# Decode attention with a gated MLP: order and pieces of the last loads, and where wo's rows are placed and multiplied

## The chip, the cores and the metric

One core of a Trainium2 chip runs the kernel. The metric is the device time of one execution in microseconds. A core has TensorE (PE; its weight loads are listed apart as PEld), VectorE (DVE), ScalarE (ACT), GpSimd (POOL) and SyncE (SP), each with its own instruction stream, and sixteen DMA engines that move data from HBM. Transfers that SP issues go through one queue (q1 in the profile), those that GpSimd issues through another (q0); both are served by the same sixteen engines.

## The reference

One token is decoded. Attention has 32 heads of 128 with 4096 cached keys and values each; beside it runs an MLP with a squared ReLU, and a sigmoid gate mixes the two. All tensors are bfloat16.

```python
g = sigmoid((x * gate_w).sum(-1, keepdims=True))          # x: 1 x 512
q = (x @ wq).reshape(1, 1, 32, 128).transpose(0, 2, 1, 3) # wq: 512 x 4096
p = softmax(einsum("bhqd,bhkd->bhqk", q, k) * 128**-0.5)  # k: 32 x 4096 x 128
o = einsum("bhqk,bhkd->bhqd", p, v)                       # v: 32 x 4096 x 128
a = o.transpose(0, 2, 1, 3).reshape(1, 1, 4096) @ wo      # wo: 4096 x 512
h = relu(x @ w1 + b1) ** 2                                # w1: 512 x 1376
b = h @ w2 + b2                                           # w2: 1376 x 512
out = g * a + (1 - g) * b
```

Keys and values are 32 MB each; with the weights, 78 MB are read for one row of 512 outputs.

## The kernel before

**Tiles and loads.** Four heads make one tile: `k_v` and `v_v` give each of NT = 8 tiles as 128 partitions of 32 KB (32 partitions a head, 128 key or value rows in each partition). A ring of SLOTS = 5 buffers of that size holds them. LOADS (L125) is the order: k0, k1, then k two tiles ahead of v, and ahead of v7 a slot "m" for what is used at the end (w1, w2, the last rows of wo). SP issues the loads in this order (L318 to L343), each after `free` (L300) has seen the slot's last reader finish. The v tiles in PARTS are issued in pieces, each with a semaphore of its own: v6 in four, v7 in four unequal ones. Behind them come the last 512 rows of wo (`wob_sb`, two transfers, L339) and the last 128 rows of w2 (`w2b`, L341). The wait in `pv` for the pieces is at L542.

**Scores, softmax, values.** Of the 128 blocks of a k tile VectorE multiplies and sums 80 (`ttr`, L711); the others are transposed on TensorE (L509), evacuated by ScalarE (L415) and multiplied on TensorE (L522). The maximum goes through `max_rows`, `gmax` and `max_cols` (L529, L725, L728, L534), ScalarE takes the exponentials (L434), and `pv` (L553) multiplies the values block by block. `den`, `recip` and `norm` divide by the sum. A loop over NU = 32 units (four to a tile) interleaves these by hand on every engine.

**wo.** Its first 3584 rows (28 heads) are loaded in mid-run into W, in the place of wq: a chunk is 32 rows of wo, 32 KB, in one partition, and 112 of the 128 partitions get one. A run `(kind, e, k, r, m)` in RUNS or FIRST is a transfer of chunks to partitions p, p + st, ...: `place` (L90) gives the start, the step and the count. e, from 0 to 15, numbers the first of k neighbours in a circle of sixteen; INNER lies in partitions 32 to 95, OUTER below 32 (e < 8) and from 96 up, SEAM joins partitions 28 + r and 96 + r (e = 7 and 8), WRAP joins r and 124 + r (e = 15 and 0). RUNS are issued by GpSimd (L378), FIRST by SP ahead of the fifth load (L327). `turns` (L99) keeps a count modulo 16 of where GpSimd's next transfer starts: a transfer of k chunks moves it by k, and where a run is to start elsewhere a tiny transfer (L375) of d rows into `dm` moves it by d. FIRST's run `(OUTER, 4, 1, 3, 1)` is one chunk alone, in partition 19.

Which chunk lies in which partition is undone by the matrix `selA` (one affine_select a run, L363): at the end `turn_a` and `spread_a` (L566, L572) turn the first 28 heads' outputs into `o2A`, 32 columns in the partitions' order.

**The end.** In program order on TensorE (L649 to L667): `turn_a`, `max_rows(7)`, `spread_a`, `out_a`, which multiplies TP = 22 of the 32 columns with W (88 matmuls, L580), `max_cols(7)`, `mlp_h` (w1, 44 matmuls, L594), `den`, `mlp_out(0..9)` (w2's first 1280 rows, 40 matmuls, L605), then the four `pv` of v7 with `add_v` before the second of them, `out_b` (the last four heads, 16 matmuls, L614) and `mlp_out(10)` (4 matmuls). All of them add up in one PSUM tile, `acc`. VectorE in the meantime (`rows_v`, L763) multiplies the other TV = 10 columns with W, 512 wide, into `vsum`, with the MLP's activation in between (`mlp_bias`, `mlp`); `add_v` (L583) sums `vsum` over the partitions on TensorE. Then VectorE adds the bias (L814), TensorE transposes (L667), and SP writes the result (L343).

Of the kernel before, what the change touches and what calls it, by code (L numbers as in the profile page):

```python
# [5 lines left out]
def bass_gated_mix__gqa_block_cached__dense_activation_squared_relu__decode_kernel(  # L6
# [50 lines left out]
    for i in (28, 29, 30):  # L57
# [3 lines left out]

    PARTS = {NT - 3: [0, 64, B], NT - 2: [0, 32, 64, 96, B], NT - 1: [0, 40, 80, 116, B]}

# [10 lines left out]
    NZ = NH - NA  # L74
    TS = [0, 3, NZ]

    TV = 10
    TP = 32 - TV
    TM = 6
    INNER, OUTER, SEAM, WRAP = range(4)  # L80
    RUNS = [(INNER, 4, 12, 0, 2), (INNER, 4, 12, 1, 2),
            (OUTER, 4, 3, 0, 1), (SEAM, 7, 2, 0, 1), (OUTER, 9, 7, 0, 1), (OUTER, 4, 3, 1, 1),
            (SEAM, 7, 2, 1, 1), (OUTER, 9, 7, 1, 1), (OUTER, 4, 3, 2, 1),
            (SEAM, 7, 2, 2, 1), (OUTER, 9, 7, 2, 1),
            (SEAM, 7, 2, 3, 1), (WRAP, 15, 2, 3, 1), (OUTER, 1, 2, 3, 1)]
    FIRST = [(INNER, 0, 3, 0, 1), (INNER, 0, 3, 1, 1), (INNER, 0, 3, 2, 1), (INNER, 0, 3, 3, 1),
             (OUTER, 0, 3, 0, 1), (OUTER, 0, 3, 1, 1), (OUTER, 0, 3, 2, 1),
             (OUTER, 4, 1, 3, 1)]

    def place(kind, e, k, r, m):  # L90
        if kind == INNER:
            return 32 + 4 * e + r, 4 // m, k * m
        if kind == OUTER:
            return (4 * e if e < 8 else 64 + 4 * e) + r, 4, k
        if kind == SEAM:
            return 28 + r, 68, k
        return r, 124, k

# [22 lines left out]
    w1_v = B_w1.rearrange("(p t) n -> p (t n)", t=4)  # L121
    w2_v = B_w2[0:FG * 128, :].rearrange("(p g) n -> p (g n)", g=FG)

# [11 lines left out]
    with ctx:  # L135
# [24 lines left out]
        oA, fin4 = [held("m")[0:p, W5 + n * 128:W5 + n * 128 + 128] for n, p in enumerate((NA, 4))]  # L160
        vsum = held("k", NT - 1)[:, 0:2 * DM].bitcast(fp32)

# [19 lines left out]
        selA = sb("selA", [NA, 4, 128], bf16)  # L182
        o2f = sb("o2f", [128, TV], fp32)
        dm = sb("dm", [16, len(RUNS), 2, 6], bf16)
# [53 lines left out]
        s_l = [sem(f"s_l{i}") for i in range(SLOTS)]  # L238
        s_w = [sem(f"s_w{n}") for n in range(3)]
        s_wo = [sem(f"s_wo{n}") for n in range(len(TS) - 1)]  # L240
        s_wp = [sem(f"s_wp{n}") for n in range(len(RUNS))]
# [40 lines left out]
        s_h = sem("s_h")  # L282
        s_vs = sem("s_vs")
        s_hv = sem("s_hv")
# [32 lines left out]
        @block.sync  # L317
        def _(eng):  # L318
            for n, (kind, j) in enumerate(LOADS):
                free(eng, n)  # L320
                if n == SLOTS - 1:
                    started(eng)
                    for p, st, k, q in STRIPS[len(RUNS):]:
                        a, b = W[p:p + st * (k - 1) + 1:st, :], woa_v[q:q + k, :]
                        if k == 1:
                            a, b = [v.rearrange("p (a n) -> p a n", a=2) for v in (a, b)]
                        eng.dma_start(a, b).then_inc(s_wr, 16)  # L327
                if kind == "v" and j in PARTS:
                    for w in range(len(PARTS[j]) - 1):
                        part = slice(PARTS[j][w] * 128, PARTS[j][w + 1] * 128)  # L330
                        eng.dma_start(held("v", j)[:, part], v_v[j][:, part]).then_inc(s_vl[j, w], 16)  # L331
                elif kind in "kv":
                    eng.dma_start(held(kind, j), (k_v if kind == "k" else v_v)[j])\
                       .then_inc(s_l[n % SLOTS], 16)
                elif kind == "m":
                    eng.dma_start(held("m")[:, 0:W2], w1_v).then_inc(s_w[0], 16)
                    eng.dma_start(held("m")[:, W2:W3], w2_v).then_inc(s_w[1], 16)  # L337
            for c in range(len(TS) - 1):
                eng.dma_start(wob_sb[:, TS[c]:TS[c + 1], :], wob_v[:, TS[c]:TS[c + 1], :])\  # L339
                   .then_inc(s_wo[c], 16)  # L340
            eng.dma_start(w2b, B_w2[F - 128:F, :]).then_inc(s_w[2], 16)  # L341
            eng.wait_ge(s_f4, 1)
            eng.dma_start(out[0, 0, :].rearrange("(j p) -> j p", p=128), fin4).then_inc(s_out, 16)  # L343
# [110 lines left out]
        def _(eng):  # L454
# [11 lines left out]
            for n in range(FG + 1):  # L466
                mm = eng.matmul(B1[:, n:n + 1], b1r[:, n:FG * 128:FG] if n < FG else b1r[:, F - 128:F],
                                ident[0:1, 0:1], start=True, stop=True)
            mm.then_inc(s_b1, 1)
# [67 lines left out]
            def pv(u):  # L537
                j, w = u // U, u % U
                lo, hi = w * B // U, (w + 1) * B // U
                if j == NT - 1:  # L540
                    lo, hi = PARTS[j][w:w + 2]
                if j in PARTS:  # L542
# [32 lines left out]

            def out_a():
                eng.wait_ge(s_ac, 2)
                for t in range(TP):
                    for j in range(4):
                        eng.matmul(acc[:, j:j + 1], wo_sb[:, t, j * 128:(j + 1) * 128], o2A[:, t:t + 1],  # L580
                                   start=(t == 0 and j == 0), stop=False, skip_group_check=True)

            def add_v():  # L583
                eng.wait_ge(s_vs, TV)
                for j in range(4):
                    eng.matmul(acc[:, j:j + 1], vsum[:, j * 128:(j + 1) * 128], onesf[:, 0:1],
                               start=False, stop=False, skip_group_check=True)

            def mlp_h():
                eng.wait_ge(s_w[0], 16)  # L590
                for n in range(FG + 1):
                    for t in range(4):
                        lhs = w1_sb[:, t, n:FG * 128:FG] if n < FG else w1_sb[:, t, F - 128:F]
                        mm = eng.matmul(H[:, n:n + 1], lhs, xcol[:, t:t + 1],  # L594
                                        start=(t == 0), stop=(t == 3))
                mm.then_inc(s_h, 1)

            def mlp_out(n):
                if n in (0, FG):
                    eng.wait_ge(s_w[1 if n < FG else 2], 16)  # L600
                if n == 0:
                    eng.wait_ge(s_hs, 1)
                w = w2a[:, n, :] if n < FG else w2b
                for j in range(4):
                    mm = eng.matmul(acc[:, j:j + 1], w[:, j * 128:(j + 1) * 128], hs[:, n:n + 1],  # L605
                                    start=False, stop=(n == FG), skip_group_check=True)
                if n == FG:
                    mm.then_inc(s_acc, 1)

            def out_b(c):  # L610
                eng.wait_ge(s_wo[c], 16)
                for h in range(TS[c], TS[c + 1]):
                    for j in range(4):
# [37 lines left out]
            spread_a()  # L651
            out_a()
            max_cols(NT - 1)
            mlp_h()
            den(NG - 1)
            for n in range(FG):
                mlp_out(n)
            for u in range((NT - 1) * U, NU):
                if u == NU - 3:
                    add_v()  # L660
                pv(u)
            eng.wait_ge(s_on, NG)
            for c in range(len(TS) - 1):
                out_b(c)
            mlp_out(FG)
            eng.wait_ge(s_fin, 1)
# [4 lines left out]
        def _(eng):  # L671
# [90 lines left out]

            def rows_v():  # L763
                eng.wait_ge(s_ac, 3)
                eng.wait_ge(s_sd, NU)
                eng.wait_ge(s_t, 2 * NU)
                eng.wait_ge(s_wk, 1)
                for t in range(TV):
                    if t == TM:
                        mlp_bias()  # L770
                        mlp()
                    if t == 0:
                        eng.tensor_scalar(vsum[:, :], wo_sb[:, TP, :], o2f[:, 0:1], None, ALU.mult)\
                           .then_inc(s_vs, 1)
                    else:
                        eng.wait_ge(s_vs, t)
                        eng.scalar_tensor_tensor(out=vsum[:, :], in0=wo_sb[:, TP + t, :],
                                                 scalar=o2f[:, t:t + 1], in1=vsum[:, :],
                                                 op0=ALU.mult, op1=ALU.add).then_inc(s_vs, 1)

            for c in range(EARLY - 1):
# [24 lines left out]
            eng.tensor_copy(o2A[:, :], O2A).then_inc(s_ac, 1)  # L806
            eng.tensor_copy(o2f[:, :], O2A[:, TP:32]).then_inc(s_ac, 1)
            gmax(NT - 1)
            rows_v()
            recip(NG - 1)  # L810
# [37 lines left out]
```

## Time and profile before

| what | value |
|---|---|
| three runs | 192.72, 192.87, 193.0 us, median 192.87 |
| the profiled execution | 192.9 us, of which the page's span is 191.5 |
| bytes moved | 78.74 MB, mean 411 GB/s |
| granted TensorE clock over the run | 0.581 |
| VectorE: `ttr` (L711) | 656 multiply-reduces of 280 ns and 656 accumulator reads of 76 ns; last one ends at 172.4 us |
| VectorE: `rows_v` (L773, L777) | 174.31 to 183.07 us, 0.49 us and nine of 0.75 us |
| SP: issue of v7's pieces, wob, w2b | 150.6 to 174.9 us |
| GpSimd: 14 runs of wo and 7 tiny transfers | issued 33.8 to 46.1 us, last one landed at 112.8 |
| one packet on a DMA engine, 32 KB | 1.213 us |
| 16 KB, 10 KB, 9 KB, 8 KB | 0.611, 0.387, 0.349, 0.310 us |
| 3 KB, 1 KB, a semaphore's 4 bytes | 0.121, 0.046, 0.009 us |

The span is what the hardware profiler saw of the kernel's instructions; the execution's own time has 1.4 us around it. A packet is one contiguous piece of one partition. The slices of the page are a fortieth of the span, 4.8 us, each; a digit is the busy share in tenths. Busy times in a table by stages are followed by the number of instructions.

### The profile page before, as it was taken

How to read it: one execution, taken by the hardware profiler on the slowest of the kernel's cores; microseconds unless marked ns; L12 is line 12 of the kernel's file. 1: busy time of each engine (PE TensorE's matmuls, PEld its weight loads, DVE VectorE, ACT ScalarE, POOL GpSimd, SP SyncE). 2: the span in 40 equal slices, each digit the busy share in tenths (PEclk: the TensorE clock that was granted, in tenths of full speed). 3: DMA queues.
4: the chain of work that ended last, by engine and by line, in shares of the span. 5: the costliest groups of instructions: out<-in, count | busy, mean ns of one | idle time of the engine just before them, and what ended most of it. 6: DMA issues, size and time to landing. Idle time of an engine off the chain costs nothing.

```text
span 191.5 us, 6005 instructions
## 1 busy us (share of the span) xinstructions
PE 111.0 (58%) x2058; PEld 97.6 (51%) x2058; DVE 159.0 (83%) x1387; ACT 82.7 (43%) x204; POOL 22.7 (12%) x56
## 2 busy tenths in 40 slices
PE   0129667545614653397569145933887478648975
PEld 0123335535503542297459145933877268537964
DVE  0320399999999999899999998998999799998821
ACT  2105765843833663087349222941663393000400
POOL 7760000996000000000000000000000000000000
PEclk9999985855555555555555555555555555555555
DMA  6999999999999999999999999999999999999992
GB/s 226 432 438 438 438 440 428 438 411 450 411 443 411 421 412 421 438 429 431 414 447 421 428 426 428 431 417 424 428 419 424 411 428 409 421 415 428 417 382 70
DMA packets 5488, 78.74 MB, mean 411 GB/s; under 512 B 1285, under 2 KB 1927, under 8 KB 2056
## 3 DMA queue, kind: packets, MB, share of 16 engines
q1 hardware_dynamic: 4484, 75.40, 92.9%
q0 software_dynamic: 960, 2.95, 3.9%
q8 instruction: 16, 0.26, 0.6%
q14 instruction: 14, 0.11, 0.1%
q10 hardware_dynamic: 14, 0.01, 0.0%
HBM read 78.35 MB, written 0.00 MB: 409 GB/s over the span
## 4 chain that ended last, share of the span: by engine, by line
DVE 48%; DMA 40%; SPq 7%; PE 3%; issue 1%; DVEq 0%
DVE ring L711 45%; DMA ring<-in_A_k_cache_dram 26%; DMA ring<-in_A_wo_dram 14%; SPq L331 6%; DVE S L711 2%; PE pO L553 1%; PE KP L509 1%; DVE gm L725 1%; DVE gx L728 0%; PE pM L562 0%; PE pM L534 0%; PE pQ L614 0%; SPq L337 0%; SPq L294 0%; DVE mp L718 0%
## 5 line engine op out<-in xcount | busy, mean ns | idle before, releaser
L711 DVE CUSTOM_DVE_ANT_0 ring<-ring,qb 128x128 bf16<-128x128 bf16 x656 | 140.6, 280 | 2.9 <-DMA ring<-in_A_k_cache_dram 2.9
L415 ACT ACTIVATE kT<-KP 128x768 bf16<-128x768 bf16 (+1 forms) x64 | 46.4, 783 | 48.1 <-PE KP L509 47.8
L509 PE MATMUL KP<-ident,ring 128*128 128x128 bf16 x368 | 43.4, 302 | 23.2 <-DMA ring<-in_A_k_cache_dram 19.9
L711 DVE DVE_READ_ACCUMULATOR2_ANT S<- 128x1 f32 x656 | 49.7, 76 | 0.1
L509 PEld LDWEIGHTS KP<-ident,ring 128*128 128x128 bf16 x368 | 36.0, 140 | 25.9 <-DMA ring<-in_A_k_cache_dram 20.4
L553 PE MATMUL pO<-E,ring 128*128 128x4 bf16 x640 | 19.5, 167 | 2.9 <-DMA ring<-in_A_v_cache_dram 1.9
L553 PEld LDWEIGHTS pO<-E,ring 128*128 128x128 bf16 x640 | 18.7, 105 | 3.4 <-DMA ring<-in_A_v_cache_dram 2.1
L434 ACT ACTIVATE E<-S,nM 32x128 bf16<-32x128 f32 x32 | 18.5, 580 | 0.9
L553 PE MATMUL pX<-E,ring 128*128 128x4 bf16 x384 | 12.0, 167 | 4.6 <-DMA ring<-in_A_v_cache_dram 4.6
L553 PEld LDWEIGHTS pX<-E,ring 128*128 128x128 bf16 x384 | 11.4, 105 | 5.1 <-DMA ring<-in_A_v_cache_dram 4.9
L426 ACT ACTIVATE nM<-pM 128x1 f32<-128x1 f32 x8 | 1.4, 172 | 23.0 <-PE pM L534 23.0
L529 PE MATMUL pM<-identf,mp 128*1 128x128 f32 x8 | 3.1, 384 | 13.0 <-DVE mp L718 13.0
L534 PE MATMUL pM<-onesf,gx 1*128 1x1 f32 x16 | 4.6, 357 | 8.9 <-DVE gx L728 8.9
L534 PEld LDWEIGHTS pM<-onesf,gx 1*128 1x128 f32 x16 | 4.0, 306 | 9.6 <-DVE gx L728 9.6
L522 PE MATMUL pQ<-qcol,kT 128*128 128x4 bf16 x176 | 7.8, 170 | 1.0 <-ACT kT L415 0.9
L522 PEld LDWEIGHTS pQ<-qcol,kT 128*128 128x128 bf16 x176 | 7.6, 111 | 1.4 <-ACT kT L415 1.4
L434 ACT ACTIVATION_READ_ACCUMULATOR E<-S,nM 32x1 f32 x32 | 8.1, 253 | 0.0
L522 PE MATMUL pS<-qcol,kT 128*128 128x4 bf16 x192 | 8.1, 169 | 0.0
L386 POOL MEMSET tick<- 1x1 f32 x1 | 0.1, 88 | 66.8 <-DMA W<-in_A_wo_dram 66.8
L378 POOL DMA_DIRECT2D W<-in_A_wo_dram x14 | 8.0, 572 | 0.0
L529 PEld LDWEIGHTS pM<-identf,mp 128*1 128x1 f32 x8 | 0.7, 92 | 14.2 <-DVE mp L718 14.0
L522 PEld LDWEIGHTS pS<-qcol,kT 128*128 128x128 bf16 x192 | 7.8, 108 | 0.2
(83 smaller groups left out, 97.3 us busy)
## 6 DMA issues: line engine op xcount, KB each, us to landing
ring<-in_A_k_cache_dram SPq DMA_DIRECT2D x8, 4096.0 KB, 30.4
ring<-in_A_v_cache_dram SPq DMA_DIRECT2D x5, 4096.0 KB, 29.7
W<-in_A_wq_dram SPq DMA_DIRECT2D x1, 4096.0 KB, 12.4
ring<-in_A_v_cache_dram SPq DMA_DIRECT2D x2, 2048.0 KB, 27.7
ring<-in_A_v_cache_dram SPq DMA_DIRECT2D x4, 1024.0 KB, 27.5
ring<-in_A_v_cache_dram SPq DMA_DIRECT2D x2, 1280.0 KB, 31.4
W<-in_A_wo_dram POOLq DMA_DIRECT2D x2, 768.0 KB, 17.8
ring<-in_B_w_dram SPq DMA_DIRECT2D x1, 1376.0 KB, 24.8
```

Of the source, the lines that this page charges most:

```text
L331: eng.dma_start(held("v", j)[:, part], v_v[j][:, part]).then_inc(s_vl[j, w], 16)
L378: eng.dma_start(W[p:p + st * (k - 1) + 1:st, :], woa_v[q:q + k, :], max_dma_last_dim=16384).then_inc(s_wp[n], 16)
L415: eng.activation(kT[:, n % NC, 0:HB[u // U] * 128], KP[n % 3][:, 0:HB[u // U] * 128], ACT.Copy).then_inc(s_ev, 1)
L426: eng.activation(nM[:, j:j + 1], MB[:, j:j + 1], ACT.Copy).then_inc(s_nm, 1)
L434: eng.activation(E[rows, j % NE, :, r], S[rows, j % NS, :], ACT.Exp, bias=nM[rows, j:j + 1], scale=SCALE, accum_out=RS[rows, R * j + r:R * ...
L509: mm = eng.transpose(KP[n % 3][:, y * 128:(y + 1) * 128], held("k", j)[:, b * 128:(b + 1) * 128], ident[:, :])
L522: mm = eng.matmul(S2[j % 2][:, c:c + R], kT[:, n % NC, y * 128:(y + 1) * 128], qcol[:, R * j:R * j + R], start=True, stop=True)
L529: eng.transpose(MT[0:1, :], mp[:, j:j + 1], identf[:, :]).then_inc(s_mt, 1)
L534: eng.matmul(MB[:, j:j + 1], gx[0:1, j % 2, :], onesf[0:1, 0:1], start=True, stop=True).then_inc(s_mb, 1)
L553: mm = eng.matmul(O(R * j, R * j + R), held("v", j)[:, b * 128:(b + 1) * 128], E[:, j % NE, b, :], start=(b == 0), stop=(b == B - 1), skip ...
L711: ins = eng.tensor_tensor_reduce(kb, kb, qb[:, j, :], 1.0, 0.0, ALU.mult, ALU.add, S[:, j % NS, b:b + 1])
L725: eng.tensor_reduce(g, MT[0:1, :].rearrange("a (r p) -> a r p", r=R), AX.X, ALU.max)\
```

## The change

Five things change, and nothing of what is computed.

- **Order and pieces of the last loads.** w1 stays ahead of v7. w2's first 1280 rows come behind v7 and behind wob, and in two transfers, of 8 and of 2 groups of 128 rows, each with its semaphore; then the last 128 rows as before. wob is one transfer. v6 and v7 come in two pieces, 96 and 32 blocks.
- **TensorE's order at the end.** The first 8 columns of `out_a`, `max_cols(7)`, the other 24 columns, `mlp_h`, `den`, the four `pv` of v7 in equal quarters, `out_b`, and then all of `mlp_out`.
- **wo's rows.** VectorE's part of them (`rows_v`, `vsum`, `o2f`) and `add_v` go; `out_a` multiplies all 32 columns (128 matmuls).
- **Chunks.** RUNS has ten runs instead of fourteen (88 chunks instead of 90), FIRST has eight of three chunks each instead of seven and a single one (24 instead of 22). WRAP and the single chunk go.
- **w1's and w2's groups.** A column of H belongs to w2's new groups: `group(n)` gives the columns of w1 and b1 (stride 8 for n < 8, stride 2 for the next two, the last 128 as before).

```diff
-    PARTS = {NT - 3: [0, 64, B], NT - 2: [0, 32, 64, 96, B], NT - 1: [0, 40, 80, 116, B]}
+    PARTS = {NT - 3: [0, 64, B], NT - 2: [0, 96, B], NT - 1: [0, 96, B]}
+
+    FE = 8
...
     RUNS = [(INNER, 4, 12, 0, 2), (INNER, 4, 12, 1, 2),
-            (OUTER, 4, 3, 0, 1), (SEAM, 7, 2, 0, 1), (OUTER, 9, 7, 0, 1), (OUTER, 4, 3, 1, 1),
-            (SEAM, 7, 2, 1, 1), (OUTER, 9, 7, 1, 1), (OUTER, 4, 3, 2, 1),
-            (SEAM, 7, 2, 2, 1), (OUTER, 9, 7, 2, 1),
-            (SEAM, 7, 2, 3, 1), (WRAP, 15, 2, 3, 1), (OUTER, 1, 2, 3, 1)]
+            (OUTER, 4, 4, 0, 1), (OUTER, 8, 8, 0, 1), (OUTER, 4, 4, 1, 1), (OUTER, 8, 8, 1, 1),
+            (OUTER, 4, 4, 2, 1), (OUTER, 8, 8, 2, 1),
+            (OUTER, 3, 2, 3, 1), (SEAM, 7, 2, 3, 1)]
     FIRST = [(INNER, 0, 3, 0, 1), (INNER, 0, 3, 1, 1), (INNER, 0, 3, 2, 1), (INNER, 0, 3, 3, 1),
-             (OUTER, 0, 3, 0, 1), (OUTER, 0, 3, 1, 1), (OUTER, 0, 3, 2, 1),
-             (OUTER, 4, 1, 3, 1)]
+             (OUTER, 0, 3, 0, 1), (OUTER, 0, 3, 1, 1), (OUTER, 0, 3, 2, 1), (OUTER, 0, 3, 3, 1)]
+
+    def group(n):
+        a, b, s = ((0, FE * 128, FE) if n < FE else (FE * 128, FG * 128, FG - FE) if n < FG else
+                   (F - 128, F, 1))
+        return slice(a + (n if n < FE else n - FE if n < FG else 0), b, s)
...
-    w2_v = B_w2[0:FG * 128, :].rearrange("(p g) n -> p (g n)", g=FG)
+    w2_v = [B_w2[a * 128:b * 128, :].rearrange("(p g) n -> p (g n)", g=b - a) for a, b in ((0, FE), (FE, FG))]
...
                 elif kind == "m":
                     eng.dma_start(held("m")[:, 0:W2], w1_v).then_inc(s_w[0], 16)
-                    eng.dma_start(held("m")[:, W2:W3], w2_v).then_inc(s_w[1], 16)
-            for c in range(len(TS) - 1):
-                eng.dma_start(wob_sb[:, TS[c]:TS[c + 1], :], wob_v[:, TS[c]:TS[c + 1], :])\
-                   .then_inc(s_wo[c], 16)
-            eng.dma_start(w2b, B_w2[F - 128:F, :]).then_inc(s_w[2], 16)
+            eng.dma_start(wob_sb, wob_v).then_inc(s_wo, 16)
+            for c, (a, b) in enumerate(((0, FE), (FE, FG))):
+                eng.dma_start(held("m")[:, W2 + a * DM:W2 + b * DM], w2_v[c]).then_inc(s_w[1 + c], 16)
+            eng.dma_start(w2b, B_w2[F - 128:F, :]).then_inc(s_w[3], 16)
...
             spread_a()
-            out_a()
+            out_a(0, TM)
             max_cols(NT - 1)
+            out_a(TM, 32)
             mlp_h()
             den(NG - 1)
-            for n in range(FG):
+            for u in range((NT - 1) * U, NU):
+                pv(u)
+            out_b()
+            for n in range(FG + 1):
                 mlp_out(n)
-            for u in range((NT - 1) * U, NU):
-                if u == NU - 3:
-                    add_v()
-                pv(u)
-            eng.wait_ge(s_on, NG)
-            for c in range(len(TS) - 1):
-                out_b(c)
-            mlp_out(FG)
...
             eng.tensor_copy(o2A[:, :], O2A).then_inc(s_ac, 1)
-            eng.tensor_copy(o2f[:, :], O2A[:, TP:32]).then_inc(s_ac, 1)
             gmax(NT - 1)
-            rows_v()
+            mlp_bias()
+            mlp()
             recip(NG - 1)
             norm(NG - 1)
```

TM is 8 after the change. `mlp_out(n)` waits for its piece of w2 at n = 0, 8 and 10, and `out_b` for the norm and for wob.

More of the change, by code (lines that the diff above doesn't have):

```diff
@@ L74, in bass_gated_mix__gqa_block_cached__dense_activation_squared_relu__decode_kernel @@
     NZ = NH - NA
[L75 to L80, printed above, removed]
+    TM = 8
+    INNER, OUTER, SEAM = range(3)
     RUNS = [(INNER, 4, 12, 0, 2), (INNER, 4, 12, 1, 2),
-            (OUTER, 4, 3, 0, 1), (SEAM, 7, 2, 0, 1), (OUTER, 9, 7, 0, 1), (OUTER, 4, 3, 1, 1),
-            (SEAM, 7, 2, 1, 1), (OUTER, 9, 7, 1, 1), (OUTER, 4, 3, 2, 1),
-            (SEAM, 7, 2, 2, 1), (OUTER, 9, 7, 2, 1),
-            (SEAM, 7, 2, 3, 1), (WRAP, 15, 2, 3, 1), (OUTER, 1, 2, 3, 1)]
+            (OUTER, 4, 4, 0, 1), (OUTER, 8, 8, 0, 1), (OUTER, 4, 4, 1, 1), (OUTER, 8, 8, 1, 1),
+            (OUTER, 4, 4, 2, 1), (OUTER, 8, 8, 2, 1),
+            (OUTER, 3, 2, 3, 1), (SEAM, 7, 2, 3, 1)]
     FIRST = [(INNER, 0, 3, 0, 1), (INNER, 0, 3, 1, 1), (INNER, 0, 3, 2, 1), (INNER, 0, 3, 3, 1),
-             (OUTER, 0, 3, 0, 1), (OUTER, 0, 3, 1, 1), (OUTER, 0, 3, 2, 1),
-             (OUTER, 4, 1, 3, 1)]
+             (OUTER, 0, 3, 0, 1), (OUTER, 0, 3, 1, 1), (OUTER, 0, 3, 2, 1), (OUTER, 0, 3, 3, 1)]
[3 more added lines that the diff above has]
+        return slice(a + (n if n < FE else n - FE if n < FG else 0), b, s)
     def place(kind, e, k, r, m):
@@ L94, in place @@
             return (4 * e if e < 8 else 64 + 4 * e) + r, 4, k
-        if kind == SEAM:
-            return 28 + r, 68, k
-        return r, 124, k
+        return 28 + r, 68, k
     def turns():
@@ L160, in bass_gated_mix__gqa_block_cached__dense_activation_squared_relu__decode_kernel @@
         oA, fin4 = [held("m")[0:p, W5 + n * 128:W5 + n * 128 + 128] for n, p in enumerate((NA, 4))]
-        vsum = held("k", NT - 1)[:, 0:2 * DM].bitcast(fp32)
         start = ring[:, SLOTS - 1, :]
@@ L182, in bass_gated_mix__gqa_block_cached__dense_activation_squared_relu__decode_kernel @@
         selA = sb("selA", [NA, 4, 128], bf16)
-        o2f = sb("o2f", [128, TV], fp32)
         dm = sb("dm", [16, len(RUNS), 2, 6], bf16)
@@ L238, in bass_gated_mix__gqa_block_cached__dense_activation_squared_relu__decode_kernel @@
         s_l = [sem(f"s_l{i}") for i in range(SLOTS)]
-        s_w = [sem(f"s_w{n}") for n in range(3)]
-        s_wo = [sem(f"s_wo{n}") for n in range(len(TS) - 1)]
+        s_w = [sem(f"s_w{n}") for n in range(4)]
+        s_wo = sem("s_wo")
         s_wp = [sem(f"s_wp{n}") for n in range(len(RUNS))]
@@ L282, in bass_gated_mix__gqa_block_cached__dense_activation_squared_relu__decode_kernel @@
         s_h = sem("s_h")
-        s_vs = sem("s_vs")
         s_hv = sem("s_hv")
@@ L323, in _ @@
                     for p, st, k, q in STRIPS[len(RUNS):]:
[L324 to L327, printed above, removed]
+                        eng.dma_start(W[p:p + st * (k - 1) + 1:st, :], woa_v[q:q + k, :]).then_inc(s_wr, 16)
                 if kind == "v" and j in PARTS:
@@ L466, in _ @@
             for n in range(FG + 1):
-                mm = eng.matmul(B1[:, n:n + 1], b1r[:, n:FG * 128:FG] if n < FG else b1r[:, F - 128:F],
-                                ident[0:1, 0:1], start=True, stop=True)
+                mm = eng.matmul(B1[:, n:n + 1], b1r[:, group(n)], ident[0:1, 0:1], start=True, stop=True)
             mm.then_inc(s_b1, 1)
@@ L539, in pv @@
                 lo, hi = w * B // U, (w + 1) * B // U
-                if j == NT - 1:
-                    lo, hi = PARTS[j][w:w + 2]
                 if j in PARTS:
@@ L574, in spread_a, with out_a @@
                 mm.then_inc(s_at, 1)
-            def out_a():
+            def out_a(a, b):
                 eng.wait_ge(s_ac, 2)
-                for t in range(TP):
+                for t in range(a, b):
                     for j in range(4):
@@ L581, in out_a @@
                                    start=(t == 0 and j == 0), stop=False, skip_group_check=True)
[L583 to L587, printed above, removed]
             def mlp_h():
@@ L592, in mlp_h @@
                     for t in range(4):
-                        lhs = w1_sb[:, t, n:FG * 128:FG] if n < FG else w1_sb[:, t, F - 128:F]
-                        mm = eng.matmul(H[:, n:n + 1], lhs, xcol[:, t:t + 1],
+                        mm = eng.matmul(H[:, n:n + 1], w1_sb[:, t, group(n)], xcol[:, t:t + 1],
                                         start=(t == 0), stop=(t == 3))
@@ L598, in mlp_out @@
             def mlp_out(n):
-                if n in (0, FG):
-                    eng.wait_ge(s_w[1 if n < FG else 2], 16)
+                if n in (0, FE, FG):
+                    eng.wait_ge(s_w[1 + (0, FE, FG).index(n)], 16)
                 if n == 0:
@@ L608, in mlp_out, with out_b @@
                     mm.then_inc(s_acc, 1)
-            def out_b(c):
-                eng.wait_ge(s_wo[c], 16)
-                for h in range(TS[c], TS[c + 1]):
+            def out_b():
+                eng.wait_ge(s_on, NG)
+                eng.wait_ge(s_wo, 16)
+                for h in range(NZ):
                     for j in range(4):
@@ L761, in mlp @@
                     eng.tensor_tensor(hs[p, n], hp[p, n], omw[p, n], ALU.mult).then_inc(s_hs, 1)
[L763 to L779, printed above, removed]
             for c in range(EARLY - 1):
```

## The prediction

> **What bounds the kernel.** I read the page first (slices, queues, chain), then a table by stages, the timeline of the end, and last what the trace keeps of each transfer: the times of its sixteen completion steps, one for each DMA engine, and the length of every packet.
>
> ```profile
> span 191.5 us, 6005 instructions
> ...
> DMA  6999999999999999999999999999999999999992
> ...
> q1 hardware_dynamic: 4484, 75.40, 92.9%
> q0 software_dynamic: 960, 2.95, 3.9%
> ...
> DVE 48%; DMA 40%; SPq 7%; PE 3%; issue 1%; DVEq 0%
> ```
>
> The chain names VectorE first, but the DMA row is full from slice 2 to slice 39. The table by stages (us, busy time of PE, PEld, DVE, ACT, POOL, then clock, DMA share, GB/s) says where that stops:
>
> ```profile
> 34.00:113.00 79.00, 40.19 (x720) 37.43 (x719) 77.67 (x714) 39.98 (x93) 12.12 (x22) 0.52 1.01 426
> 113.00:150.00 37.00, 24.95 (x552) 24.30 (x550) 35.52 (x328) 18.60 (x42) 0.02 (x1) 0.50 1.00 425
> 150.00:172.00 22.00, 14.12 (x320) 12.72 (x321) 20.99 (x195) 7.36 (x21) 0.00 (x0) 0.50 1.00 417
> 172.00:186.00 14.00, 12.45 (x283) 11.61 (x280) 9.44 (x25) 2.53 (x9) 0.00 (x0) 0.50 1.00 414
> 186.00:189.30 3.30, 2.10 (x68) 1.91 (x66) 0.22 (x1) 0.00 (x0) 0.00 (x0) 0.50 0.49 171
> ```
>
> The DMA share (column before the last) is 1.00 up to 186 and 0.49 after: the sixteen engines never starve, but they do not finish together. VectorE is nearly as busy until 172, yet transfers sit about 25 us in the queue (chain and issue rows), so it holds none of them up. The end of the timeline:
>
> ```profile
> 188.26 0.22 DVE L741 SCALAR_TENSOR_TENSOR onorm<-pO,gcol,rden 128x4 bf16<-128x4 f32 x1 [5.10 <-PE pO L553]
> 188.67 0.51 PEld L614 LDWEIGHTS pQ<-onorm,ring 128*128 128x128 bf16 x16 [0.60 <-DVE onorm L741]
> 188.70 0.57 PE L614 MATMUL pQ<-onorm,ring 128*128 128x1 bf16 x16 [0.55 <-DMA ring<-in_A_wo_dram]
> ...
> 189.26 0.27 PE L605 MATMUL pQ<-hs,ring 128*128 128x1 bf16 x4
> 189.57 0.16 DVE L814 TENSOR_TENSOR fin<-pQ,b2g 128x4 bf16<-128x4 f32 x1 [1.09 <-PE pQ L605]
> ```
>
> The last three small transfers set the end. Completion steps of the very last (w2's last 128 rows, L341), sorted, one per DMA engine:
>
> ```
> 186.46 186.74 186.78 186.82 187.26 187.31 187.73 188.00
> 188.38 188.45 188.54 188.70 188.76 188.77 188.80 189.22
> ```
>
> Fifteen engines are done by 188.80, one needs until 189.22, and the matmuls on these rows start at 189.26. So the time is that of the most loaded DMA engine plus 0.32 us of PE and then a fixed tail.
>
> **Which engine is it.** The seven three-partition strips of FIRST (L327) end in triples (53.35, 53.48, 53.51; then 54.60 and so on to 60.54, 60.72, 60.78): three engines carry seven chunks of 32 KB each. The one-partition strip leaves a single step, at 63.00: one engine carries an eighth. The loads that follow on the same queue show a straggler: last steps 72.51, 82.28, 92.66, 103.02, 112.81, 122.49 and so on, 9.7 us (eight packets of 1.213) apart at the end, where the next engine is 1.7 to 2.2 us earlier up to 113. Twice, 82.28 to 92.66 and 92.66 to 103.02, the step is 0.67 longer: the two 16 KB packets of a WRAP chunk. By the count that turns() keeps (modulo 16, GpSimd transfers one engine a chunk) WRAP lies on numbers 15 and 0. So the straggler is number 0, with nine chunks (7+1+1). The same count gives 8 chunks for 1, 2, 7, 8 and 15, none for 3, and 7 for the other nine. One track shows neither kind of chunk, and nearly every 8 KB instruction fetch (queue q14) sets it back by about 1.0 us; I take it for number 3.
>
> **The change, part by part.**
>
> Chunks. Number 0 loses the one-partition strip (1.213 us, 32 KB packet) and its WRAP part (2 x 0.611 = 1.22) and gains the fourth three-partition OUTER strip (1.213): 8 chunks, -1.22 us. Numbers 1 and 2 lose the last OUTER run and gain that strip: nothing. 15 loses one (-1.22), 3 gains its first (+1.22), 4 an eighth (+1.22). The others keep theirs. Following tracks by their equal steps, that engine ends at 186.78, so number 3 would reach 188.0 at most, harmless. Which track number 4 is, the trace does not say.
>
> Larger pieces. v6 goes from four 8 KB packets a partition (0.310 each, 1.242) to 24 KB and 8 KB; 24 KB from the line through 8 KB and 32 KB (1.213) is 0.912, so 1.222. Eight partitions an engine: -0.16. v7: 2 x 0.387 + 0.349 + 0.121 = 1.244 becomes 1.222: -0.17. w2: 10 KB 0.387 becomes 8 KB 0.310 and 2 KB, which lies between two 1 KB packets (0.092) and two thirds of a 3 KB one (0.081); I take 0.083: +0.05. Four completion packets less (2, 2 and 1 less, 1 more) at 9 ns: -0.04. Sum -0.32 us on **every** engine, whichever is last; both ends of the 2 KB price change it by under 0.1.
>
> So the former straggler would end at 189.22 - 1.22 - 0.32 = 187.68, and the next, 188.80 - 0.32 = **188.48**, is last: -0.74.
>
> The tail. After the last step there are still only four matmuls, but w2's first piece lands at the slowest engine only 8 x 0.083 + about 0.34 (L341's own spacing) = 1.0 us earlier, and its 32 matmuls follow. PE streams 88 in 2.51 us (L580), so 26.9 ns each and 0.17 for the last: 43 x 26.9 + 170 = 1.33 us, from 0.05 after that landing: last step + 0.38, against + 0.32 now. **+0.05**.
>
> PE before that. The 40 matmuls more on wo rows cost 40 x 26.9 = 1.1 us, add_v saves 1.87 and w2's 40 (1.21) move behind. VectorE loses its ten row operations (0.49 + 6.8) and o2f (0.16): nobody waits for that, since it was idle 5.10 before L741. Laid out from 173.9: 32 matmuls to 174.8, max_cols (0.58, gx ready at 174.3), 96 to 178.1, mlp_h 2.60 (its weights now read at stride 8 and 2 for 10; at L580's contiguous pace 1.3, I keep the slow end) to 180.7, den 0.59 (the exps, 2.4 us after max_cols, are done by 178.2) to 181.3. v7's 24 KB part lands about 173.9 + 7.3 = 181.2; 96 matmuls to 184.0, the 8 KB part (183.7) to 185.0, norm with its waits 0.55 (pO's end 188.15 to 188.70), out_b 0.57 to 186.2. w2's first piece lands at 187.5. Cover 1.3 us; all of this costs nothing, and if the cover went, whatever exceeds it would be added whole. v6's last part is used to 172.35 as now (96 matmuls from 168.65, 32 from 171.45). On SP one transfer is added behind wob and five left out: nothing waits, as w2's last lies 14 us in the queue. On GpSimd 18 selects for 22 (0.47 each) before it idles 19.6 us, and 17 issues for 21 (about 0.58) 66 us ahead of its next wait: nothing.
>
> **Sum**: -0.74 + 0.05 = -0.69 us on a profiled 192.9 (span 191.5 and 1.4 around it), 0.03 over the median of 192.87: **192.2 us**.
>
> [...] The added small transfer: the last two, 128 KB each, end 0.33 us apart, the price of their packets. [...] The instruction fetches: PE's 16 KB fetches at 138.0, 145.2, 151.8, 161.9, 168.0, 177.5 and 184.1 each set one engine back by 1.5 us, a different one each time, and that at 188.4 set back none that mattered. [...]
>
> **Rivals.**
>
> 1. *Number 4 becomes the straggler* (slower). Its new chunk is 1.22 us; if its track was one of the five that end at 188.70 to 188.80, it ends at 189.6 to 189.7: 0.4 to 0.5 later than now, 193.3 to 193.4. It decides from a track ending above about 188.6. Against: 7-chunk engines should be the earlier group (six end by 187.73). For: at least three of the late group must be 7-chunk engines set back by late fetches. Chance 0.2.
>
> 2. *The balance only shifts*: number 4 at 188.38 to 188.54 gives 189.3 to 189.4, so 193.0 to 193.1. Chance 0.08.
>
> 3. *A fetch moves*: PE's stream is 64 instructions longer before the tail, so the fetch of 188.4 comes about 2 us earlier, while engines still work. On one that ended by 187.3 it is harmless; on that of 188.00 it gives 188.0 - 0.32 + 1.5 = 189.2, so 192.9. Chance 0.12.
>
> 4. *PE becomes the bound, or the added transfer is not hidden*: 193 for half a microsecond over the cover; 194 if the transfer costs what the result's write does, 1.2 us from issue to landing. It would need a stall that no row shows. Chance 0.04.
>
> 5. *The code's count is wrong*, so that number 0 keeps an extra chunk: only the -0.32 and the +0.05 are left, 192.6. The single step at 63.00 speaks against it. Chance 0.04.
>
> **From these to numbers.** The forecast has 0.52. A measurement can tell about 0.2%, 0.39 us, so below 192.48 is faster and above 193.26 slower. Faster: forecast and a little of 3, 0.55. Slower: 1 and 4, 0.23. Same: the rest, 0.22. The forecast's own range is 191.8 (last step 188.06, if the late group thins to its lowest) to 192.5; with the rivals 191.8 to 193.4.
>
> **What would show it.** Right: last step of w2's last transfer near 188.5 with several engines within 0.3 us; v6 and v7 parts 7.3 and 2.5 us apart at one engine; PE waiting for w2's first piece, not the piece for PE; GpSimd issuing 17 transfers. Wrong: one engine alone at the end again, 0.5 us or more behind the rest (rival 1 or 2), PE still in v7 or wo when w2's first piece lands (4), or a last step after 189.2.

## The result, and the profile after

The change made the kernel slower: 193.81 us (median of six runs, 193.66 to 194.61) beside 192.95 us before, a ratio of 1.0052 with a 95% interval of 1.0037 to 1.0066. Four of the six runs lie at 193.7 to 193.8, two near 194.5; the profiled one is of the second kind, 194.46. A second measurement later had all its runs at 194.3 to 194.8.

The page of the changed kernel, its span and its chain:

```profile
span 193.1 us, 6038 instructions
...
DVE 59%; DMA 25%; PE 11%; issue 4%; SPq 0%; DVEq 0%
```

Before, the chain ran through the loads to the very end. Now PE and "issue", time in which an engine waits for nothing that the profile shows, have 15% of it. In this profile the loads end nearly where they were forecast to. Steps of w2's last transfer, one per DMA engine:

```
185.23 186.51 186.66 186.78 186.94 187.23 187.54 188.06
188.28 188.34 188.42 188.47 188.56 188.57 188.59 188.63
```

No engine stands alone at the end, as the one at 189.22 did before, and the last step is at 188.63; 188.48 was forecast. But TensorE ends w2's matmuls only at 191.08, 2.45 us after that step; before, it ended at 189.53, 0.31 us after. Its timeline from 173 on (start, length, instruction, count, and in brackets the idle time before it):

```profile
173.33 0.72 PE L570 MATMUL pQ<-o2A,W 128*128 128x1 bf16 x21 [0.29 <-DVE o2A L768]
174.85 0.43 PE L570 MATMUL pQ<-o2A,W 128*128 128x1 bf16 x11 [0.80 <-issue]
175.22 0.58 PE L526 MATMUL pM<-onesf,gx 1*128 1x1 f32 x2
175.73 2.72 PE L570 MATMUL pQ<-o2A,W 128*128 128x1 bf16 x96
178.31 1.29 PE L577 MATMUL pX<-xcol,ring 128*128 128x1 bf16 x19
181.32 1.23 PE L577 MATMUL pX<-xcol,ring 128*128 128x1 bf16 x25 [1.72 <-issue]
182.41 0.57 PE L552 MATMUL pM<-RS,onesf 128*128 128x4 f32 x2
182.84 2.83 PE L543 MATMUL pO<-E,ring 128*128 128x4 bf16 x101
188.05 0.88 PE L543 MATMUL pO<-E,ring 128*128 128x4 bf16 x27 [2.37 <-issue]
189.32 0.58 PE L598 MATMUL pQ<-onorm,ring 128*128 128x1 bf16 x16 [0.40 <-DVE onorm L721]
189.77 1.31 PE L588 MATMUL pQ<-hs,ring 128*128 128x1 bf16 x44
```

Three waits of 0.80, 1.72 and 2.37 us stand in the middle of runs of equal matmuls, with no semaphore to wait for. Count what lies between them: 11 + 2 + 96 + 19 = 128 and 25 + 2 + 101 = 128. With its weight load a matmul is two instructions (2090 of each in the trace), so 128 are 256 instructions; q8, a queue of kind "instruction" in the profile, moved 0.26 MB in 16 packets of 16 KB, by my estimate from these counts 64 bytes for each of the 256. I call such a set of instructions a block. In the count of all matmuls of the trace the waits stand ahead of numbers 1746, 1874 and 2002. q8's packets start at 172.5, 178.8, 185.5 and 189.4, and each wait ends 2.3 to 2.5 us after one of the first three. I read that as TensorE having run out of instructions; the runs with moved blocks, below, test it.

The kernel before had one such wait too, where it cost nothing (1.58 us of waiting for VectorE follow):

```profile
145.27 1.45 PE L553 MATMUL pO<-E,ring 128*128 128x4 bf16 x49
147.72 0.56 PE L553 MATMUL pO<-E,ring 128*128 128x4 bf16 x15 [1.00 <-issue]
```

It ends 2.54 us after the fetch of 145.2 that the prediction lists. So the sign stood in the profile before the change. In the tail of that kernel the same three blocks begin inside these rows, without such a wait:

```profile
173.88 2.51 PE L580 MATMUL pQ<-o2A,W 128*128 128x1 bf16 x88 [0.28 <-DVE o2A L806]
180.19 1.21 PE L605 MATMUL pQ<-hs,ring 128*128 128x1 bf16 x40
186.71 1.44 PE L553 MATMUL pO<-E,ring 128*128 128x4 bf16 x48 [0.66 <-DMA ring<-in_A_v_cache_dram]
```

What sets the packet's time shows when the two kernels are put side by side (us):

| block begins at matmul | 1618 | 1746 | 1874 | 2002 |
|---|---|---|---|---|
| before: TensorE reaches it | 164.6 | 174.5 | 180.5 | 187.1 |
| before: packet of the next block | 168.0 | 177.5 | 184.1 | 188.4 |
| after: TensorE reaches it | 168.9 | 174.85 (waited) | 181.32 (waited) | 188.05 (waited) |
| after: packet of the next block | 172.5 | 178.8 | 185.5 | 189.4 |

In these rows the packet follows 3.0 to 4.2 us after the block ahead of it has begun, while the loads run (DMA share 1.00 to 1.01 from 150 to 186 in both kernels), and 1.3 to 1.4 us after as they run out (last column; 0.49 and 0.37 from 186 to 189.3). The whole traces have 2058 and 2090 matmuls, sixteen times 128 and a rest, and sixteen packets of q8 each. So my reading of these times is that the next block is asked for when the present one begins and queues behind the loads. From one block's start to the next's the changed kernel needs 5.9 to 6.7 us; 128 matmuls at 26.9 ns take 3.4.

### The profile page after: what moved, and what is told of

Read it like the earlier page. It is cut to its first block, busy times and chain, and to the rows that moved or that the text cites. A ratio compares the mean times of both kernels' runs of the same rounds, so it can differ in the third digit from the quotient of the medians.

```text
span 193.1 us, 6038 instructions
## 1 busy us (share of the span) xinstructions
PE 108.6 (56%) x2090; PEld 96.1 (50%) x2090; DVE 151.6 (79%) x1376; ACT 82.6 (43%) x204; POOL 18.5 (10%) x48
## 4 chain that ended last, share of the span: by engine, by line
DVE 59%; DMA 25%; PE 11%; issue 4%; SPq 0%; DVEq 0%
DVE ring L691 54%; DMA ring<-in_A_k_cache_dram 25%; DVE S L691 2%; PE pQ L570 2%; PE pO L543 2%; PE KP L501 1%; PE pX L577 1%; PE pX L543 1%; PE pM L552 1%; PE pQ L588 1%; PE pM L526 1%; DVE gm L705 1%; DVE onorm L721 0%; DVE gx L708 0%; PE pQ L514 0%
## 5 line engine op out<-in xcount | busy, mean ns | idle before, releaser
L691 DVE DVE_READ_ACCUMULATOR2_ANT S<- 128x1 f32 x656 | 52.1, 79 | 0.1
L543 PE MATMUL pX<-E,ring 128*128 128x4 bf16 x384 | 11.5, 166 | 5.0 <-DMA ring<-in_A_v_cache_dram 5.0
L399 ACT ACTIVATE qb<-pQ 32x128 bf16<-32x128 f32 x16 | 4.3, 268 | 7.8 <-PE pQ L479 7.5
```

Source lines behind the costliest of these rows:

```text
L399: eng.activation(qb[rows, c, :], QR[c % 2][rows, r * 128:r * 128 + 128], ACT.Copy)\
L543: mm = eng.matmul(O(R * j, R * j + R), held("v", j)[:, b * 128:(b + 1) * 128], E[:, j % NE, b, :], start=(b == 0), stop=(b == B - 1), skip ...
L691: ins = eng.tensor_tensor_reduce(kb, kb, qb[:, j, :], 1.0, 0.0, ALU.mult, ALU.add, S[:, j % NS, b:b + 1])
```

## The experiments

All ratios are to the kernel before, on the same chip; medians are in us. e1 to e4 ran on one chip, e5 to e8 on a second, e9 to e12 on a third, and the changed kernel's second time beside e14 on a fourth, so across these groups the ratios are to be compared.

| run | median | ratio, 95% interval |
|---|---|---|
| changed kernel, first and second time | 193.81, 194.64 | 1.0052 (1.0037 to 1.0066), 1.0084 (1.0070 to 1.0097) |
| e1, 36 idle matmuls at the start | 192.78 | 0.9996 (0.9988 to 1.0005) |
| e2, 64 | 192.71 | 0.9992 (0.9983 to 1.0001) |
| e5, 16 | 194.61 | 1.0084 (1.0068 to 1.0100) |
| e6, 128 | 194.62 | 1.0082 (1.0067 to 1.0097) |
| e3, v6 in four pieces | 193.28 | 1.0016 (1.0007 to 1.0025) |
| e4, before with the new chunks | 192.64 | 0.9984 (0.9975 to 0.9993) |
| e7 and e14, changed with the old chunks | 194.71, 194.76 | 1.0089 (1.0074 to 1.0104), 1.0095 (1.0081 to 1.0108) |
| e8, changed with w2 ahead of v7 | 195.04 | 1.0114 (1.0091 to 1.0136) |
| e9, changed with ten columns of wo's rows on VectorE | 193.39 | 1.0016 (1.0004 to 1.0028) |
| e10, before with v6 in two pieces | 192.94 | 1.0001 (0.9992 to 1.0010) |
| e11, e9 with v6 in four pieces | 192.94 | 1.0006 (0.9997 to 1.0015) |
| e12, e10 with new chunks and 36 idle matmuls | 192.60 | 0.9981 (0.9971 to 0.9990) |

### Moving the blocks: e1, e2, e5, e6

```diff
             eng.wait_ge(s_id, 4)
+            for _ in range(36):      # 64, 16, 128
+                eng.matmul(pS[:, 511:512], ident[:, :], ident[:, 0:1], start=True, stop=True)
             eng.wait_ge(s_b, 32)
```

> The changed kernel with 36 idle matmuls (into an unused PSUM column) on TensorE at the start, while it waits for the first loads. Nothing in the tail differs but where the 16 KB blocks of TensorE's instructions (128 matmuls with their weight loads) begin: at matmuls 1710, 1838 and 1966 of the old count instead of 1746, 1874 and 2002. Fetch theory (a block is asked for when the one before it begins, and is there about 6.5 us later, so a dense tail starves): 1582 is now passed before the wait for v6 at 163, so the block at 1710 is there in time, the next two come at about 178 and 184.5, before v7 has been multiplied, and the waits of 1.72 and 2.37 us go: the end is the loads', about 2 us earlier in the profiled run, 192.0 to 192.7 us. Work theory (the added matmuls and w2 behind v7 are simply too much for TensorE): no change, 193.6 to 194.5. Chunk theory (wo's new places slow the loads): no change either.

> The same with 64 idle matmuls. Blocks then begin at 1682, 1810, 1938 and 2066 of the old count, and the last lies 24 matmuls ahead of the end. Fetch theory: 1938 begins at about 184, its successor is there only about 6 us later, at 190, with 24 matmuls and the tail behind it: little or no gain over the changed kernel, 193.3 to 194.3, and a wait near the end, inside w2's matmuls. If instead any idle matmul at the start helps (a warmer clock, say), it is as fast as with 36. Work and chunk theories: no change from the changed kernel.

> The changed kernel with 16 idle matmuls at the start. Blocks of instructions begin at 1730, 1858 and 1986 of the old count; the block of 1730 is asked for at 1602, which still lies behind the wait for v6 (1591). Fetch theory: the waits stay and move 16 matmuls towards the front, with 104 instead of 88 matmuls behind the last: as slow as the changed kernel or up to 0.6 us slower, 193.6 to 195. If any idle matmul at the start helps, it is near 192.7 as with 36 and 64.

> The changed kernel with 128 idle matmuls at the start, exactly one block. Fetch theory: every block begins at the same matmul of the tail as in the changed kernel, so the same waits come back at the same places (21 matmuls into wo's rows, 19 into w1's, 101 into v7's): 193.5 to 194.6. If idle matmuls help by themselves, four times as many as with 36 help no less: 192.7.

36 matmuls more, and the loss is gone. The tail of e1:

```profile
173.56 1.02 PE L572 MATMUL pQ<-o2A,W 128*128 128x1 bf16 x32 [0.29 <-DVE o2A L770]
174.51 0.58 PE L528 MATMUL pM<-onesf,gx 1*128 1x1 f32 x2
175.02 2.72 PE L572 MATMUL pQ<-o2A,W 128*128 128x1 bf16 x96
177.60 2.40 PE L579 MATMUL pX<-xcol,ring 128*128 128x1 bf16 x44
...
181.65 3.57 PE L545 MATMUL pO<-E,ring 128*128 128x4 bf16 x128 [1.22 <-DMA ring<-in_A_v_cache_dram]
185.68 0.57 PE L600 MATMUL pQ<-onorm,ring 128*128 128x1 bf16 x16 [0.46 <-DVE onorm L723]
188.07 1.33 PE L590 MATMUL pQ<-hs,ring 128*128 128x1 bf16 x44 [1.82 <-DMA ring<-in_B_w_dram]
```

In the tail no matmul waits for "issue" any more; one wait of 1.22 us for a block stands at 164.06 instead, ahead of a wait of 3.7 us for v6, where it costs nothing. TensorE waits for v7 and then, for 1.82 us, for w2, as the prediction had laid it out. With 128, one whole block, the waits stand where they were. The tail of e6:

```profile
175.15 0.43 PE L572 MATMUL pQ<-o2A,W 128*128 128x1 bf16 x10 [0.81 <-issue]
...
181.62 1.21 PE L579 MATMUL pX<-xcol,ring 128*128 128x1 bf16 x24 [1.65 <-issue]
...
188.32 0.86 PE L545 MATMUL pO<-E,ring 128*128 128x4 bf16 x27 [2.37 <-issue]
```

So idle matmuls do not help as such (nor by the clock: the mean granted one is 0.588 in the profiled run of e1 and 0.584 in those of e6 and of the changed kernel), and the work of the tail is not too much as such: its place against the blocks decides. e5 was slow, as expected. e2 was a miss: it came out as fast as e1, though a block begins 24 matmuls ahead of its end:

```profile
187.85 1.44 PE L590 MATMUL pQ<-hs,ring 128*128 128x1 bf16 x44 [1.83 <-DMA ring<-in_B_w_dram]
```

Its last packet started at 185.9, 3.5 us after the block ahead began, and TensorE reached the place only at 188.5, since it had waited 1.83 us for w2. The wait for data left the late block its time in this run; I had counted none.

With the waits gone, what is left of the change is small: 0.9996 and 0.9992 of the kernel before, 0.1 to 0.2 us, where the prediction had 0.69 from the loads. e1 lies 0.08 us above its range.

### Undoing parts: e3, e4, e7, e14, e8

e3 is `NT - 2: [0, 32, 64, 96, B]` in PARTS of the changed kernel; e4 has RUNS, FIRST and place() as in the change, in the kernel before; e7 and e14 are the reverse. e8 moves the w2 transfers and matmuls:

```diff
                     eng.dma_start(held("m")[:, 0:W2], w1_v).then_inc(s_w[0], 16)
+                    for c, (a, b) in enumerate(((0, FE), (FE, FG))):
+                        eng.dma_start(held("m")[:, W2 + a * DM:W2 + b * DM], w2_v[c]).then_inc(s_w[1 + c], 16)
...
             den(NG - 1)
+            for n in range(FG):
+                mlp_out(n)
             for u in range((NT - 1) * U, NU):
                 pv(u)
             out_b()
-            for n in range(FG + 1):
-                mlp_out(n)
+            mlp_out(FG)
```

> The changed kernel with v6 in four pieces as before (v7 still in two). Fetch theory: TensorE passes matmul 1618 near 164.8 instead of 168.9, so the block of 1746 is there when the tail reaches it and the wait of 0.80 us goes; the next two blocks still come 6.5 us after one another (180.5, 187.1), so 0.7 to 1.0 us of the changed kernel's loss comes back, 192.7 to 193.4, though the loads carry 0.16 us more of packets. Work theory and chunk theory: no change, or 0.16 slower.

> The kernel before with RUNS, FIRST and place() of the change alone. My sum for the loads: DMA engine 0 loses a chunk (1.22 us), the next engines in line were 0.42 us earlier, so the last landing moves by 0.4 us at most, to about 188.8, and the end with it: 192.4 to 192.6; with engine 4 as a new straggler 192.9 to 193.3. Chunk theory (the new places are what made the changed kernel slower): 193.5 or more.

> The changed kernel with RUNS, FIRST and place() of before. Fetch theory: DMA engine 0 is again the straggler, some 0.4 us behind the rest, but TensorE ends 2 us after the last landing and does not see it: 193.5 to 194.5, no difference from the changed kernel. Chunk theory (the new places cost something): 192.9 to 193.2.

> The changed kernel with w2's two larger pieces loaded ahead of v7, and mlp_out(0..9) ahead of the values on TensorE, as before; all rows of wo stay on TensorE and v6 and v7 stay in two pieces. Fetch theory: the block of 2002 still begins about 188.0 with the same 88 matmuls behind it, whatever they are: 193.4 to 194.5. Order theory (w2 behind v7 leaves 44 matmuls for the end): the 40 matmuls leave the end, 192.7 to 193.1.

> The changed kernel once more, beside the next on the same chip. Its six runs lay at 193.7 to 193.8 and 194.5 to 194.6, and the runs with 128 idle matmuls and with the old chunks lay at 194.6 alone. Fetch theory: the same waits at 1746, 1874 and 2002; if the levels come from how long one block takes, the profile has them longer or shorter by as much as the time differs: 193.6 to 194.7.

> The changed kernel with the old chunks, on the same chip as the changed kernel. Fetch theory: equal within 0.3 us, since TensorE ends 2 us after the last landing in both. Chunk theory turned round (the new chunks save 0.4 us here too): 0.3 to 0.5 us slower than the changed kernel.

e3 gave back some 0.4% or more (1.0016 for 1.0052 and 1.0084), and the wait at 1746 is gone from its trace; the other two remain:

```profile
178.90 1.40 issue
...
184.64 2.38 issue
187.01 0.90 PE pO L543 x27
```

This is the chain of e3. Its last block begins at 187.01 instead of 188.05: the chain of blocks starts earlier because TensorE passes matmul 1618 with v6's first piece, at 164.1, and not behind the long wait for v6 (5.02 us, 163.16 to 168.18, in the changed kernel, where 1618 comes at 168.9).

e4 is faster than the kernel before, by 0.16%: last landing 188.86 against 189.22 in one profile of each, 0.36 us where 0.42 was the forecast's room. Inside the changed kernel the chunks are worth nothing that can be measured: e14 and the changed kernel beside it on one chip are 194.76 and 194.64. e8 speaks against the order as the cause: with w2's 40 matmuls out of the end it is not faster (195.04, the slowest of all), its last block beginning at 188.4 with 89 matmuls behind it:

```profile
180.35 1.23 PE L577 MATMUL pX<-xcol,ring 128*128 128x1 bf16 x25 [1.45 <-issue]
188.41 1.96 PE L543 MATMUL pO<-E,ring 128*128 128x4 bf16 x68 [2.08 <-issue]
```

The packet between these two started at 185.92, 5.6 us after 180.35, where the table of the two kernels has 3.0 to 4.2; why is not shown. e7 and e8 are 0.2 and 0.5 us above their ranges.

### Fewer matmuls in the tail: e9, e10, e11, e12

e9 puts `o2f`, `vsum`, `rows_v` and `add_v` back and `out_a` to 22 columns:

```diff
-            out_a(TM, 32)
+            out_a(TM, TP)
...
             for u in range((NT - 1) * U, NU):
+                if u == NU - 3:
+                    add_v()
                 pv(u)
```

e11 is e9 with v6 in four pieces; e10 is the kernel before with `NT - 2: [0, 96, B]`; e12 is e10 with the chunks of e4 and the 36 matmuls of e1.

> The changed kernel with wo's last ten columns on VectorE again (rows_v, o2f, vsum, add_v with 4 matmuls), so 36 matmuls fewer in TensorE's tail (32 fewer in the profile's count, an f32 matmul counting twice); v6 in two pieces, w2 behind v7. Fetch theory: the blocks of 1746, 1874 and 2002 still begin about 174.8, 181.3 and 188.0, but 56 matmuls instead of 88 lie behind the last: about 1.3 us earlier than the changed kernel, 192.5 to 193.4. If the work on TensorE were the bound, 36 matmuls of 27 ns are 1.0 us, much the same; the place of the waits tells.

> As the run with the rows on VectorE, and v6 in four pieces as well: what is left of the change is the order of the loads at the end, v7 in two pieces and the chunks. Fetch theory: 1746 begins about 173.9, 1874 about 180.4, 2002 about 186.9, with 55 matmuls behind it: all in place when w2's last pieces land, so the end is the loads', 192.5 to 192.9. Order theory (w2 behind v7 costs by itself): 193.2 or more.

> The kernel before with one line changed: v6 in two pieces of 96 and 32 blocks instead of four. It moves less through the queue (0.16 us fewer on every DMA engine). Fetch theory: TensorE now waits for v6 until 168.2 ahead of matmul 1618, asks for the next block 4 us later than before, and waits about 0.5 us at 1746 and some 1 us at 2002, where 56 matmuls, the norm and the tail follow: 193.3 to 193.9, about as slow as the whole change. Packet theory (larger pieces are only cheaper): 192.7 to 192.8.

> A candidate: the kernel before with the new chunks, v6 in two pieces, and 36 idle matmuls at the start so that the blocks begin at 1710, 1838 and 1966 of the old count and the next lies behind the end (2058 + 36 < 2130). Fetch theory: no wait of TensorE's is left, the loads are 0.4 (chunks) and 0.16 us (pieces) earlier: 192.3 to 192.6, at or below the chunks alone (192.64). Without a fetch effect the same.

e9 gives back most of the loss and e11 nearly all (its interval includes no change). In e9's tail only the wait at 1746 is left (0.64 us, ending at 174.83): the next two blocks begin at 181.9 and 188.3, behind waits for v7 (1.49 us) and for VectorE's rows (0.76 us), and its chain runs through those rows. e11, with v6 in four pieces as well, has no such wait in its tail. That fits two causes that make the chain of blocks late, the longer run of matmuls and the later start. e9's runs fall into two groups, 192.7 to 193.0 and 193.4 to 193.75.

e10 was a miss: 192.94, no loss. Its trace has the packet of the next block at 172.6 instead of 168.0, as expected, but VectorE's sums ended at 172.66 instead of 172.19 in that execution (172.4 in the table of the kernel before is too late), TensorE came to wo's rows at 174.37 instead of 173.88, met the block there, and then ran through v7 without the wait of 0.66 us that the kernel before has at 186.05:

```profile
185.34 2.93 PE L553 MATMUL pO<-E,ring 128*128 128x4 bf16 x88
```

That kernel has room for some half a microsecond; I had priced the wait at 2002 at 1 us. So in these runs merging v6 did harm only together with the longer tail.

e12 is the fastest run, 0.19% below the kernel before, not to be told from e4: v6 in two pieces, priced at 0.16 us, shows nothing here, as in e10. e4, e6 and e11 lie above their ranges by less than 0.05 us.

## Why the prediction was wrong

**What bounds the kernel, the straggler, the chunks**: right in the main. The chunks alone gained 0.16% (e4), 0.3 us, and in e4 and in the first profile of the changed kernel no other engine took the straggler's place as rivals 1 and 2 had it. But with the same chunks one engine again ends 0.34 to 0.49 us behind the rest in four other profiles (the changed kernel's second, e5, e9 and e12); which one it is, and why, stays open.

**Larger pieces, 0.32 us**: mis-sized, and the last step's 188.63 for 188.48 is luck. Seven profiles have the changed kernel's loads (both of its own, e1, e2, e5, e6 and e9); their last steps lie between 188.63 and 189.16, at 188.95 in the mean, and 188.63 is the earliest. The kernel before has one profile, 189.22. With the old chunks (e7, e14) they are at 188.96 and 188.99. The time of all packets, divided by sixteen engines, is 186.68 us in e4 and 186.55 and 186.61 in the changed kernel: 0.07 to 0.13 less, not 0.32. Part of it is that packets of 1 KB took 0.048 us in the mean instead of 0.046, and those of 2 KB 0.088 instead of 0.083; the rest is not traced further.

**The tail, +0.05**: right where the loads set the end; in e1 the matmuls end 0.42 us after the last landing of 189.00, for 0.38. The added transfer was hidden behind the queue, as forecast: in the changed kernel's profile it ends 0.63 us after the piece ahead of it (187.67 to 188.30), and its eight packets on an engine take 0.7.

**"PE before that ... Cover 1.3 us; all of this costs nothing"**: this step failed, and it turned the gain into a loss. I laid the tail's matmuls end to end at 26.9 ns, a rate read from a run of 88 whose instructions were there in time, and asked of each only whether its data had landed. out_b was to be done by 186.2 and was at 189.9. mlp_h, at the pace I allowed for, was to end at 180.7 and ended at 182.5. In place of the cover stand the waits of 0.80, 1.72 and 2.37 us, and moving the blocks alone takes the loss away (e1, e2) and brings it back (e6). The price is missing from the sum: in the profile the last step comes 0.59 us earlier and the span from there to its end is 2.1 us longer, so that the span grew by 1.55 us. Without this step's failure the forecast would still have been too low, by the term of the loads above: e1 and e2 gained 0.1 to 0.2 us of the 0.69, and their 192.78 and 192.71 lie above the forecast's own range of 191.8 to 192.5.

**v6 in two pieces "used to 172.35 as now"**: the data, yes (to 171.76); but behind the wait of 5.02 us ahead of it matmul 1618 begins at 168.9 instead of 164.6 and the next block's packet starts at 172.5 instead of 168.0, and e3 shows v6 in two pieces to cost some 0.4% at least.

**The rivals**: the fourth named TensorE, at 0.04, since "no row shows" a stall; the wait of 1.00 us at 147.72 in the kernel before is such a row. Its sign came true, TensorE still in v7 (to 188.93) when w2's first piece had landed (187.67). One of its prices does not follow from its terms: 192.2 and 1.2 us make 193.4, not 194. The third had the fetches, but only the 1.5 us that they set a DMA engine back, not how late they come while the loads run (3.0 to 4.2 us after the block ahead has begun): in this tail TensorE waited 0.80, 1.72 and 2.37 us at three block starts, 4.9 us together.

**Open**: why the changed kernel has two levels 0.8 us apart, one chip showing only the upper. The two profiles that I have of it are both of the upper, with waits of 0.80 and 0.38, 1.72 and 1.99, and 2.37 and 2.38 us. What asks for a block is not shown; that it is the start of the block ahead is my reading of the times.

## What to carry to other kernels

Here a dense stretch of small matmuls was, by my reading, bounded by how fast its instructions came: with the DMA engines full up to 186 (a share of 1.00 to 1.01 from 150 on), the changed kernel needed 5.9 to 6.7 us from one block's start to the next, where 128 matmuls at 26.9 ns would take 3.4. Where a chain shows "issue" in the middle of a run of equal instructions, count the instructions between two such waits, and compare them with the starts of the instruction queue's packets; look for such waits before the change too, also where they cost nothing. A long wait just ahead of such a stretch made it worse here: without the 5.02 us for v6, e3 lost 0.16% where the changed kernel lost 0.52 and 0.84. Moving the blocks by a few idle instructions is a cheap test; here 36 matmuls undid the loss (0.9996), without a gain worth the name.

The other half of the lesson is that one profile is a thin base for the end of the loads: the last step of the same loads moved by half a microsecond from profile to profile, nearly as much as the change was to gain.

## What the runs showed of the hardware

For the blocks of matmuls 1618, 1746 and 1874 in the two kernels' profiles, the next 16 KB packet of q8 starts 3.0 to 4.2 us after TensorE has begun the block, while the loads run, and for that of 2002 1.3 to 1.4 us after, as they run out (187.1 to 188.4, 188.05 to 189.4). In the changed kernel's tail the packets of 172.5, 178.8 and 185.5 took 1.06 to 1.08 us, and the matmul at which TensorE waited ran 2.3 to 2.5 us after the packet's start.
